# Attention beside a Fourier mix in one kernel: bursts of 6, 5 and 5 key chunks, half sums kept in DRAM, query tiles that stay in place

## The chip, the cores and the metric

The kernel runs on one core of a Trainium2 chip. The time is device microseconds (us) of one execution; the number compared is the median of several executions. Lower is better. The engines are named as in the profile: PE (TensorE matmuls; PEld its weight loads), DVE (VectorE), ACT (ScalarE), POOL (GpSimd) and SP (SyncE, which here only issues DMAs; its queue is written SPq).

## The reference

Two parts that share nothing; the output sets them side by side.

```python
# A: 2048 rows, D = 1024, 32 query heads of 32, one key head and one value head
q = (x @ wq) as 32 heads;  k = x @ wk;  v = x @ wv
p = softmax(q @ k.T * 32 ** -0.5)
a = concat_heads(p @ v) @ wo
# B: real part of a 2-D Fourier transform by matrices
re = xb @ dft_hid_re.T;  im = xb @ dft_hid_im.T
b = dft_seq_re @ re - dft_seq_im @ im
out = concatenate([a, b], axis=-1)          # 2048 x 2048
```

## The kernel before

**Attention.** A unit `u` is 512 queries times 4 heads; there are 32 units. A unit takes 32 steps in each of two passes. The score pass (`score_step`) computes a 128 x 1024 block of scores a step into `pss` (two buffers of the PSUM memory that PE writes), DVE takes its row maxima (`nm<-pss`) and ACT its exponentials and row sums. The second pass (`expo`), 44 steps behind, computes the scores again with keys on the partitions into `pst` (one buffer), and ACT writes their exponentials to a `p` tile: two `p` tiles for each chunk of 128 keys. A **burst** (`pv`) then multiplies several chunks' `p` tiles by the values: per chunk four matmuls with 32 columns of `v`, side by side in the PE array, into a `psb` bank. DVE adds the bank to the unit's sum `ov`. Before, every fourth chunk starts a burst: four of them a unit, at steps 8, 16, 24 and 32 (which is step 0 of the next unit).

**Products.** Everything else that PE multiplies (the query projections, the Fourier part in two stages, the output projection) is a list of `Group`s of float32 products, each split in three matmuls of reduced-precision halves: `rh,mh`, `rl,mh`, `rh,ml`. `take(n)` issues the next n of these matmuls; between the score and exp matmuls of each step `level` takes as many as bring the fill position `pos["fill"]` to its goal at the next burst. So a step is two `pss`, two `pst` and some product matmuls (five or six as a rule); a step with a burst takes none, except the few that `aside` needs to leave an opened or nearly closed group.

**Operands.** Left operands (`m`) and right operands (`r`) run through a `Line` of four steps: load from DRAM (on SP), sum of up to three sources (`comb`: POOL, `m<-m,m` and `r<-r,r`), high half (`mh`, `rh`: POOL cast), low half (`ml`, `rl`: POOL subtraction). `lead` says how many fill positions before its due time each step is issued; right operands had (40, 40, 14, 8). Right operands of a set are due one by one over the set before.

**The Fourier part's second stage** (`stage2`) works through `PRODUCTS`: seven products of summed blocks. Each is 16 groups of 24 product matmuls: eight row blocks `k` for the first half of the contraction, then eight for the second. A row of `PRODUCTS` holds the left operand's sources, the right operand's, and the outputs to which the product is added. The first half's result stayed in an SBUF tile `h` until the second half's group added to it (DVE, `h<-h,psb`); then POOL adds it to each output that exists already (`y<-y,h`, the earlier value having been loaded from DRAM) and SP stores it; an output's first value is stored as it is.

**Order.** `Ordered` records each engine's instructions in the order of the program, so an engine that waits holds up all that is behind it; SP is such a queue too. `open_unit` opens the next unit's query tile `qst` six steps ahead: a POOL memset of its last 32 partitions and three loads.

## Time and profile before

| | |
|---|---|
| three runs | 2765.34 us median, 2764.76 to 2766.59 |
| the profiled execution | 2764.96 us, of which the span from first to last instruction is 2762.9 us |
| granted TensorE clock | 1.000 |
| busy: PE / PEld / DVE / ACT / POOL | 2750.9 / 1927.0 / 1599.3 / 2173.0 / 1650.2 us |
| DMA | 458 MB, 166 GB/s in the mean |

Everything runs through one helper line (L66), so groups are told apart by their tiles: `out<-in`. Matmuls overlap in the pipeline: a row's duration is longer than the distance to the next start, and this distance is what a matmul costs PE. A float32 matmul of a burst is two instructions in the trace; a burst of four chunks is 4 x 4 x 2 = 32.

### The profile page before, as it was taken

Reading aid. Unit: us, or ns where it says so; the run is one execution under the profiler, and the core shown is the slowest. Engines: PE = TensorE matmul, PEld = TensorE weight load, DVE = VectorE, ACT = ScalarE, POOL = GpSimd, SP = SyncE. Lnnn points to the kernel's source line nnn. Section 1 sums busy time; section 2 is a strip of 40 time slices with the busy share of each in tenths; the row PEclk is TensorE's granted clock in tenths of the full one; section 3 lists DMA queues with packets and bytes.
Section 4 is the critical chain, followed back from the end, with each engine's and each line's share of the span. In section 5 each row is a group of like instructions: output and inputs, shape, how many; then the busy total and the mean of one; then the engine's idle time right before and its main releaser. Section 6 shows DMA issues by size and latency. Waiting matters only on the chain.

```text
span 2762.9 us, 39957 instructions
## 1 busy us (share of the span) xinstructions
PE 2750.9 (100%) x13868; PEld 1927.0 (70%) x13868; DVE 1599.3 (58%) x1830; ACT 2173.0 (79%) x3131; POOL 1650.2 (60%) x1620
## 2 busy tenths in 40 slices
PE   9999999999999999999999999999999999999999
PEld 6767676766767676676767677666676767677667
DVE  5766666666666665555555565555565555556411
ACT  3588788888888888888888888878888888888741
POOL 4845525655536447767785576798887885640110
PEclk9999999999999999999999999999999999999999
DMA  7643336765675555554463454555555552554455
GB/s 270 196 130 121 123 99 196 235 221 186 208 246 196 168 164 164 154 164 139 148 189 111 127 165 126 182 191 162 170 182 150 173 166 79 162 159 140 123 168 179
DMA packets 302473, 458.01 MB, mean 166 GB/s; under 512 B 31040, under 2 KB 96320, under 8 KB 302272
## 3 DMA queue, kind: packets, MB, share of 16 engines
q1 hardware_dynamic: 301120, 453.50, 52.7%
q8 instruction: 109, 1.79, 0.3%
q10 hardware_dynamic: 1152, 1.97, 0.2%
q14 instruction: 92, 0.75, 0.1%
HBM read 349.44 MB, written 104.60 MB: 164 GB/s over the span
## 4 chain that ended last, share of the span: by engine, by line
PE 97%; POOL 1%; DMA 1%; DVE 1%; issue 0%; ACT 0%; SPq 0%; POOLq 0%; ACTq 0%; DVEq 0%
PE psb L66 60%; PE pss L66 19%; PE pst L66 17%; POOL y L66 0%; DVE nm L66 0%; SPq L66 0%; DMA u<-y 0%; DVE y L66 0%; ACT p L66 0%; DMA p<-in_xT_dram 0%; POOL ml L66 0%; DMA m<-in_cT_dram 0%; DMA r<-s 0%; ACT pss L66 0%; POOL rl L66 0%
## 5 line engine op out<-in xcount | busy, mean ns | idle before, releaser
L66 DVE TENSOR_REDUCE nm<-pss 128x1 f32<-128x1024 f32 x1024 | 1252.5, 1223 | 576.8 <-PE pss L66 576.3
L66 ACT ACTIVATE p<-pst 128x1024 f32<-128x1024 f32 x1026 | 1052.7, 1026 | 457.9 <-PE pst L66 453.9
L66 ACT ACTIVATE pss<-pss,nm 128x1024 f32<-128x1024 f32 x1024 | 1112.3, 1086 | 63.1 <-DVE nm L66 61.1
L66 PE MATMUL psb<-rh,ml 128*128 128x512 f32 x1806 | 711.2, 394 | 3.7 <-POOL ml L66 3.7
L66 PE MATMUL psb<-rh,mh 128*128 128x512 f32 x1806 | 710.9, 394 | 0.4 <-ACT rh L66 0.4
L66 PE MATMUL psb<-rl,mh 128*128 128x512 f32 x1806 | 709.9, 393 | 0.8 <-DVE rl L66 0.8
L66 PE MATMUL pss<-kst,qst 128*128 128x512 f32 x2048 | 657.4, 402 | 0.1
L66 PE MATMUL pst<-qst,kst 128*128 128x512 f32 x2048 | 648.3, 397 | 0.9 <-ACT p L66 0.7
L66 PEld LDWEIGHTS pss<-kst,qst 128*128 128x128 f32 x2048 | 372.5, 188 | 182.9 <-issue 99.7
L66 PE MATMUL psb<-p,v 128*32 128x512 f32 x4096 | 466.0, 596 | 0.8 <-DVE y L66 0.8
L66 POOL TENSOR_TENSOR ml<-m,mh 128x512 fp32r<-128x512 f32 x338 | 436.3, 1291 | 33.8 <-ACT mh L66 26.4
L66 PEld LDWEIGHTS pst<-qst,kst 128*128 128x128 f32 x2048 | 379.4, 188 | 104.4 <-ACT p L66 16.0
L66 PEld LDWEIGHTS psb<-rh,ml 128*128 128x128 f32 x1806 | 339.4, 188 | 83.9 <-POOL ml L66 5.6
L66 PEld LDWEIGHTS psb<-rh,mh 128*128 128x128 f32 x1806 | 339.4, 188 | 82.9 <-ACT rh L66 2.1
L66 PEld LDWEIGHTS psb<-rl,mh 128*128 128x128 f32 x1806 | 339.4, 188 | 80.8 <-DVE rl L66 1.7
L66 POOL TENSOR_TENSOR r<-r,r 128x512 f32<-128x512 f32 x112 | 144.4, 1289 | 302.2 <-DMA r<-s 158.7
L66 PEld LDWEIGHTS psb<-p,v 128*32 128x32 f32 x4096 | 120.4, 110 | 276.7 <-issue 262.1
L66 POOL CAST mh<-m 128x512 fp32r<-128x512 f32 x337 | 206.4, 612 | 158.8 <-PE psb L66 141.2
L66 POOL CAST rh<-r 128x512 fp32r<-128x512 f32 x208 | 127.7, 614 | 249.9 <-PE psb L66 159.7
L66 POOL TENSOR_TENSOR rl<-r,rh 128x512 fp32r<-128x512 f32 x208 | 268.6, 1292 | 3.9
L66 POOL TENSOR_TENSOR m<-m,m 128x512 f32<-128x512 f32 x192 | 247.9, 1291 | 29.9 <-DMA m<-in_xbT_dram 21.4
L66 DVE TENSOR_TENSOR ov<-ov,psb 128x512 f32<-128x512 f32 x96 | 66.1, 688 | 288.7 <-PE psb L66 288.7
(91 smaller groups left out, 961.9 us busy)
## 6 DMA issues: line engine op xcount, KB each, us to landing
m<-in_cT_dram SPq DMA_DIRECT2D x384, 256.0 KB, 3.7
r<-s SPq DMA_DIRECT2D x192, 256.0 KB, 4.3
y<-y SPq DMA_DIRECT2D x96, 256.0 KB, 4.6
r<-in_wT_dram SPq DMA_DIRECT2D x80, 256.0 KB, 3.8
m<-in_xbT_dram SPq DMA_DIRECT2D x80, 256.0 KB, 4.1
y<-u SPq DMA_DIRECT2D x80, 256.0 KB, 2.9
m<-in_wq_dram SPq DMA_DIRECT2D x64, 256.0 KB, 3.1
qst<-qh SPq DMA_DIRECT2D x64, 256.0 KB, 5.3
```

The costliest lines, as they stand in the source:

```text
L66: return lambda *a, **k: self.tc.keep_in_program_order(f(*a, **k))
```

## The change

- `CUT = (0, 6, 11, NC)`: a unit's 16 chunks go in three bursts of 6, 5 and 5 chunks, at steps 12, 22 and 32. There are 96 bursts where there were 128. The pool of `p` tiles has 13 buffers instead of 9, and `level` spreads the product matmuls over 12 or 10 steps.
- Room for the 4 `p` tiles comes from the eight `h` tiles. The first half's sum goes to DRAM (`hs`, 56 stores) and comes back with the other old values (`part`, 56 loads, first in the list `ys`) into a `y` tile, to which DVE adds the second half.
- Third sources of a sum, which lay in `h` tiles, use the second source's two buffers (`r1`, `m1`); `may` lets an operand with three sources, and the one behind it, be loaded only when all sums before it are issued.
- Query tiles are three fixed ones. POOL clears each once (3 memsets instead of 32); for the other 29 units a DMA copies two rows of zeros over the two rows that the unit before wrote.
- `PRODUCTS`: the second row becomes the fourth.
- Right operands' sums are issued 28 positions ahead, not 40; their loads stay at 40.

```diff
 PRODUCTS = [
     ([(0, 0, 1), (1, 1, 1)], ((0, 0), (1, 1)), [(0, 0, 1), (1, 1, 1)]),
-    ([(0, 1, 1), (1, 1, 1)], ((0, 0),), [(1, 0, 1), (1, 1, -1)]),
     ([(0, 0, 1)], ((0, 1), (1, 1)), [(0, 1, 1), (1, 1, 1)]),
     ([(0, 0, 1), (1, 0, 1)], ((1, 1),), [(0, 0, 1), (0, 1, -1)]),
+    ([(0, 1, 1), (1, 1, 1)], ((0, 0),), [(1, 0, 1), (1, 1, -1)]),
...
         def may(self, k):
             if k == 0:
+                if self.n[1] < i and any(len(it.srcs) > 2 for it in self.items[i - 1:i + 1] if it.srcs):
+                    return False
...
-    RL = Line(NR0, NR, (40, 40, 14, 8), load_r, comb, hi_r, lo)
+    RL = Line(NR0, NR, (40, 28, 14, 8), load_r, comb, hi_r, lo)
...
                     if half == 0:
-                        def post(ps, k=k):
-                            hs[k] = hp.tile([P, W], F32, name=f"h{k}")
-                            dve.tensor_copy(hs[k], ps)
+                        def post(ps, k=k, hs=hs, f=f):
+                            o = op.tile([P, W], F32, name="qh")
+                            dve.tensor_copy(o, ps)
+                            store(hs[k], o, ("h", f, k))
                         yield Group(left, R, post)
                         continue
-                    ys = []
+                    part = Item([(lambda k=k, hs=hs, f=f: have(("h", f, k), hs[k]), 1)])
+                    ys = [part]
...
-                    def post(ps, k=k, plan=plan):
-                        h = hs[k]
+                    def post(ps, part=part, plan=plan):
+                        h = part.y
                         dve.tensor_add(h, h, ps)
...
-    qsp = pool(ctx, "qsp", 3)
-    pp = pool(ctx, "pp", 9)
+    qsp = pool(ctx, "qsp", 1)
+    rows = []
+    NP = 13
+    pp = pool(ctx, "pp", NP)
...
-        q = qsp.tile([P, 4, W], F32R, name="qst")
-        gp.memset(q[96:P].bitcast(F32), 0.0)
+        if u < 3:
+            rows.append(qsp.tile([P, 4, W], F32R, name=f"qst{u}"))
+            gp.memset(rows[u][96:P].bitcast(F32), 0.0)
+        q = rows[u % 3]
+        if u >= 3:
+            move(sp, q[96:98].rearrange("p a b -> p (a b)"), kst[98:100])
...
+    CUT = (0, 6, 11, NC)
...
-        for c in range(4 * k, 4 * k + 4):
+        for c in range(CUT[k], CUT[k + 1]):
...
+    ENDS = [2 * c for c in CUT]
     def level(n):
-        k, r = divmod(n, 8)
-        if r == 0:
+        r = n % SU
+        if r in ENDS:
             return
-        left = goal((k + 1) * 8) - pos["fill"]
-        take(left - left * (7 - r) // (8 - r))
+        more = min(e for e in ENDS if e > r) - r
+        left = goal(n + more) - pos["fill"]
+        take(left - left * (more - 1) // more)
...
-        if r % 8 == 0 and n:
-            pv(*divmod(n // 8 - 1, 4))
+        if r in ENDS and n:
+            pv((n - 1) // SU, (ENDS.index(r) - 1) % (len(CUT) - 1))
```

How the order of instructions changes is shown at three places. On PE, a burst in the second stage, with the step around it, before:

```order
L66 MATMUL psb<-rh,ml 128x512
L66 MATMUL psb<-ident,nm 48x128
L66 MATMUL pss<-kst,qst 128x512 x2
L66 MATMUL pst<-qst,kst 128x512 x2
L66 MATMUL psb<-p,v 32x512 x16
L66 MATMUL pss<-kst,qst 128x512 x2
L66 MATMUL pst<-qst,kst 128x512 x2
L66 MATMUL psb<-rh,mh 128x512
```

and a first burst of a unit there now:

```order
L66 MATMUL psb<-rh,ml 128x512
L66 MATMUL pss<-kst,qst_688 128x512 x2
L66 MATMUL pst<-qst_1988,kst 128x512 x2
L66 MATMUL psb<-p,v 32x512 x24
L66 MATMUL pss<-kst,qst_688 128x512 x2
L66 MATMUL pst<-qst_1988,kst 128x512 x2
L66 MATMUL psb<-rh,mh 128x512
```

The burst has 24 matmuls (6 chunks) instead of 16, and what stands around it is the same; the transposition `psb<-ident,nm`, which stood right before a unit's third burst, now stands two steps behind one.

On POOL, one group of the second half of the fourth product, before:

```order
L66 TENSOR_TENSOR y_17136<-y_17136,h_16285 128x512
L66 TENSOR_TENSOR y_17138<-y_17138,h_16285 128x512
L66 TENSOR_TENSOR m_17181<-m_17181,m_17183 128x512
L66 TENSOR_TENSOR ml<-m_17111,mh 128x512
L66 TENSOR_TENSOR r_17310<-r_17310,r_17312 128x512
L66 CAST mh<-m_17181 128x512
L66 CAST rh<-r_17176 128x512
L66 TENSOR_TENSOR m_17261<-m_17261,m_17263 128x512
L66 TENSOR_TENSOR ml<-m_17181,mh 128x512
L66 TENSOR_TENSOR rl<-r_17176,rh 128x512
L66 CAST mh<-m_17261 128x512
```

and at that place now:

```order
L66 TENSOR_TENSOR y_17104<-y_17104,y_17102 128x512
L66 TENSOR_TENSOR m_17140<-m_17140,m_17142 128x512
L66 TENSOR_TENSOR ml<-m_17078,mh 128x512
L66 CAST mh<-m_17140 128x512
L66 CAST rh<-r_17136 128x512
L66 TENSOR_TENSOR m_17188<-m_17188,m_17190 128x512
L66 TENSOR_TENSOR ml<-m_17140,mh 128x512
L66 TENSOR_TENSOR rl<-r_17136,rh 128x512
L66 TENSOR_TENSOR r_17278<-r_17278,r_17280 128x512
L66 CAST mh<-m_17188 128x512
```

One `y` addition a group is gone (the product that now stands fourth has one output that exists already; the one with two now stands third, where the next product's right operands need no sums), and the right operand's sum stands later among the left operands' steps.

On SP, the same place, before (`s` is stage one's result, `cT` the Fourier matrix):

```order
L66 DMA y_17286<-y_0_4_245 128x512
L66 DMA y_17288<-y_1_4_253 128x512
L66 DMA r_17310<-s_5_324 128x512
L66 DMA r_17312<-s_5_340 128x512
L66 DMA m_17315<-in_cT_dram 128x512
L66 DMA m_17317<-in_cT_dram 128x512
L66 DMA y_0_3_244<-y_17136 128x512
L66 DMA out_dram<-y_17138 128x512
```

and now:

```order
L66 DMA y_17212<-hs_3_407 128x512
L66 DMA y_17214<-y_1_3_268 128x512
L66 DMA qst_1316<-kst 2x2048
L66 DMA qst_1316<-qh_6_79 32x4x512
L66 DMA qst_1316<-ql_6_111 32x4x512
L66 DMA qst_1316<-qh_6_79 32x4x512
L66 DMA r_17278<-s_4_320 128x512
L66 DMA r_17280<-s_4_336 128x512
L66 DMA m_17282<-in_cT_dram 128x512
L66 DMA m_17284<-in_cT_dram 128x512
```

The half sum `hs` is loaded at the head of the group's loads, and the zeros for a query tile are a DMA ahead of its three loads.

More of the change, by code (lines that the diff above doesn't have):

```diff
@@ L132, in tile_kernel @@
     op = pool(ctx, "op", 3, side="right")
-    hp = pool(ctx, "hp", 1, side="right")
     def move(q, to, of):
@@ L184, in load_r @@
         for n, (ap, _) in enumerate(it.srcs):
-            if n < 2:
-                it.t.append(r0p.tile([P, W], F32, name=f"r{n}", bufs=NR0 - n))
-            else:
-                it.t.append(spare(0, 5))
+            k = min(n, 1)
+            it.t.append(r0p.tile([P, W], F32, name=f"r{k}", bufs=NR0 - k))
             sp.dma_start(it.t[-1], ap())
@@ L196, in load_m @@
             a = ap()
-            if n < 2:
-                t = m0p.tile([P, 4, P], F32, name=f"m{n}", bufs=NM0 - n)
-            else:
-                t = spare(5, 3).rearrange("p (a b) -> p a b", a=4)
+            k = min(n, 1)
+            t = m0p.tile([P, 4, P], F32, name=f"m{k}", bufs=NM0 - k)
             it.t.append(t[:, :a.shape[1], :a.shape[2]])
             sp.dma_start(it.t[-1], a)
-    turn = {0: 0, 5: 0}
-    def spare(first, n):
-        turn[first] += 1
-        return hp.tile([P, W], F32, name=f"h{first + turn[first] % n}")
     def comb(it):
@@ L481, in stage1 @@
                     yield Group(left, R[n], post, ys=ys, part=(R, 4 * n))
-    hs = {}
     def have(key, ap):
@@ L493, in stage2 @@
                 total[t, e] = total.get((t, e), 0) + 1
-        for mt, nt, outs in PRODUCTS:
+        for f, (mt, nt, outs) in enumerate(PRODUCTS):
+            hs = [dram.tile([P, W], F32, name=f"hs_{f}_{k}") for k in range(8)]
             for half in range(2):
@@ L690, in pv @@
         ps = bank("psb")
-        for c in range(4 * k, 4 * k + 4):
+        for c in range(CUT[k], CUT[k + 1]):
             for h in range(4):
-                te.matmul(ps[h * DH:(h + 1) * DH], v[:, c], pt[u, c, h // 2][:, h % 2], start=c == 4 * k, stop=c == 4 * k + 3)
+                te.matmul(ps[h * DH:(h + 1) * DH], v[:, c], pt[u, c, h // 2][:, h % 2], start=c == CUT[k], stop=c == CUT[k + 1] - 1)
         if k == 0:
@@ L699, in pv @@
         cur["at"] += 1
-        if k == NC // 4 - 1:
+        if k == len(CUT) - 2:
             b, g = units[u]
@@ L740, in tile_kernel @@
         te.matmul(ps_t.tile([P, 2, W], F32, name="pst")[:, 0, :n], zeros[:, :P], zeros[:, :n], start=True, stop=True)
-    room = [t[:, k] for t in [pp.tile([P, 2, W], F32, name="p") for _ in range(9)] for k in range(2)]
-    room += [hp.tile([P, W], F32, name=f"h{k}") for k in range(8)]
-    room += [t[:, k].bitcast(F32) for t in [qsp.tile([P, 4, W], F32R, name="qst") for _ in range(2)] for k in range(4)]
+    room = [t[:, k] for t in [pp.tile([P, 2, W], F32, name="p") for _ in range(NP)] for k in range(2)]
+    room += [r0p.tile([P, W], F32, name="r1", bufs=NR0 - 1) for _ in range(2)] + [onp.tile([P, W], F32, name="rb")]
+    room += [m0p.tile([P, 4, P], F32, name="m1", bufs=NM0 - 1).rearrange("p a b -> p (a b)") for _ in range(2)]
+    room += [r0p.tile([P, W], F32, name="r0", bufs=NR0)]
     xs = [[room[b * ND + c] for c in range(ND)] for b in range(NQ)]
@@ L813, in tile_kernel @@
     take(last[0].at - pos["fill"] - 12)
-    pv(len(units) - 1, 3)
+    pv(len(units) - 1, len(CUT) - 2)
     while ends:
```

## The prediction

> **What bounds the kernel.** I read the page's busy table and its chain first.

> ```profile
> span 2762.9 us, 39957 instructions
> PE 2750.9 (100%) x13868; PEld 1927.0 (70%) x13868; DVE 1599.3 (58%) x1830; ACT 2173.0 (79%) x3131; POOL 1650.2 (60%) x1620
> PE 97%; POOL 1%; DMA 1%; DVE 1%; issue 0%; ACT 0%; SPq 0%; POOLq 0%; ACTq 0%; DVEq 0%
> ```

> PE is idle for 12.0 us of the span (2762.9 - 2750.9), and 97% of the chain that ended last is PE. So an edit pays only if PE gets less to do, or if it closes one of the few waits of PE. The change leaves the number of matmuls as it is; what it can touch on PE is the cost of starting and ending a burst, and the waits. I sum against the profiled execution, 2764.96 us (2.1 us of it outside the span); the median of the runs, 2765.34, is 0.4 us above it. Under 0.2% (5.5 us) I would not tell a change from none.

> **Fewer bursts.** The timeline of PE shows a burst, then steps of six and of five product matmuls without one (start, duration, instruction; only starts matter, since matmuls overlap).

> ```profile
> 1002.48 0.63 PE L66 MATMUL pst<-qst,kst 128*128 128x512 f32 x2
> 1003.03 3.64 PE L66 MATMUL psb<-p,v 128*32 128x512 f32 x32
> 1006.60 0.73 PE L66 MATMUL pss<-kst,qst 128*128 128x512 f32 x2
> 1007.17 0.62 PE L66 MATMUL pst<-qst,kst 128*128 128x512 f32 x2
> ...
> 1009.02 0.63 PE L66 MATMUL pss<-kst,qst 128*128 128x512 f32 x2
> 1009.48 0.63 PE L66 MATMUL pst<-qst,kst 128*128 128x512 f32 x2
> 1009.95 0.40 PE L66 MATMUL psb<-rh,mh 128*128 128x512 f32 x1
> ...
> 1011.33 0.63 PE L66 MATMUL pss<-kst,qst 128*128 128x512 f32 x2
> ...
> 1013.42 0.63 PE L66 MATMUL pss<-kst,qst 128*128 128x512 f32 x2
> ```

> Two windows inside the burst show where a wave of four neighbouring matmuls starts, five waves apart; the third row, of the chain, is a longer run of column tiles (64 wide, 16 waves of two) at the kernel's start.

> ```profile
> 1003.48 1.04 PE L66 MATMUL psb<-p,v 128*32 128x512 f32 x8
> 1005.63 1.04 PE L66 MATMUL psb<-p,v 128*32 128x512 f32 x8
> 13.23 7.02 PE pss L66 x32
> ```

> A wave is (1005.63 - 1003.48) / 5 = 0.43 us, a chunk two waves, 0.86. Four chunks are 3.44. The burst costs more than that at three places. It starts 0.55 after the `pst` pair (1002.48 to 1003.03), where a product starts 0.47 after one (1009.48 to 1009.95): 0.08. From its start to the next `pss` pair 3.57 pass, 0.13 more than the eight waves. And this pair takes 0.57 (1006.60 to 1007.17) instead of 0.46 (1009.02 to 1009.48): 0.11. Together 0.32 us a burst. That the 0.13 doesn't grow with the length is shown by the 16 waves at the start: 7.02 - 16 x 0.43 = 0.14. The chunks stay 512, the bursts become 96 from 128: 32 x 0.32 = **-10.2 us**. Bounds: only the 0.08 of the entry goes (-2.6), or the whole 0.32 and a bit of unseen waiting too (0.35, -11.2). I take 0.32, because all three parts sit at a burst's ends.

> [...]

> **Longer stretches between bursts.** Nine or eleven steps now run between bursts instead of seven. A step with five product matmuls is 2.09 us (1011.33 to 1013.42), one with six 2.31 (1009.02 to 1011.33). ACT goes through the steps with five without a gap (`pss` exponentials between):

> ```profile
> 1014.55 1.02 ACT L66 ACTIVATE p<-pst 128x1024 f32<-128x1024 f32 x1
> ...
> 1016.64 1.03 ACT L66 ACTIVATE p<-pst 128x1024 f32<-128x1024 f32 x1
> ```

> Its turn is 2.09 (1014.55 to 1016.64), as long as PE's. So a step with four products could be bound by ACT. Two such steps before a burst:

> ```profile
> 1138.99 0.63 PE L66 MATMUL pst<-qst,kst 128*128 128x512 f32 x2
> 1140.86 0.63 PE L66 MATMUL pst<-qst,kst 128*128 128x512 f32 x2
> 1142.75 0.73 PE L66 MATMUL pst<-qst,kst 128*128 128x512 f32 x2
> ```

> They take 1.87 and 1.89, and only behind the second does the `pst` pair take 0.10 longer: ACT lags by one of its turns at most, and catches up in the burst. The order of the changed kernel has 41 such steps instead of 28, four times three in a row, which before has nowhere. A third one in a row may cost up to the whole 0.22 (2.09 - 1.87). Four of those, and a few more pairs at 0.10: **+1 us**. Bounds: 0, and 41 x 0.22 = +9.

> **POOL: the waits of PE that there are.** Rows of the list of waits (us in total, times, longest), of the DMA table and of the groups, a window (its length, then PE's busy time), POOL's timeline about the first wait of PE for it, and DVE's additions of half sums, one a group, where nothing jams:

> ```profile
> PE psb L66 <- POOL ml L66: 3.7, 4, 1.2
> POOL r L66 <- DMA r<-s: 158.7, 62, 8.9
> PEld pst L66 <- ACT p L66: 16.0, 67, 0.7
> r<-s SPq DMA_DIRECT2D x192, 256.0 KB, 4.3
> L66 POOL MEMSET qst<- 32x2048 f32 x32 | 57.8, 1805 | 1.8
> 1800.00:1850.00 50.00, 47.17 (x233) 32.90 (x232) 27.94 (x32) 38.87 (x57) 45.70 (x45) 1.00 0.63 201
> 1794.54 1.30 POOL L66 TENSOR_TENSOR r<-r,r 128x512 f32<-128x512 f32 x1 [4.88 <-DMA r<-s]
> 1795.77 0.61 POOL L66 CAST mh<-m 128x512 fp32r<-128x512 f32 x1
> ...
> 1801.18 2.55 POOL L66 TENSOR_TENSOR y<-y,h 128x512 f32<-128x512 f32 x2
> ...
> 1814.15 2.54 POOL L66 TENSOR_TENSOR y<-y,h 128x512 f32<-128x512 f32 x2
> ...
> 2022.68 0.69 DVE L66 TENSOR_TENSOR h<-h,psb 128x512 f32<-128x512 f32 x1 [0.38 <-PE psb L66]
> 2032.88 0.69 DVE L66 TENSOR_TENSOR h<-h,psb 128x512 f32<-128x512 f32 x1
> 2046.85 0.69 DVE L66 TENSOR_TENSOR h<-h,psb 128x512 f32<-128x512 f32 x1 [0.16 <-PE psb L66]
> ```

> PE waits four times for `ml`, 3.7 us in all; 2.8 us of its idle time lie between 1800 and 1850 (50 - 47.17): the second half of the fourth product, one operand after POOL's wait of 4.88. There POOL does per group eight sums or subtractions at 1.29 and three casts at 0.61, 12.2 us, and waits for a right operand's load besides (4.88 in the row). Two `y` pairs stand 13.0 us apart; a group of 24 products takes PE 12.1 where nothing jams (half of 2022.68 to 2046.85). POOL falls behind. The change takes one 1.29 out of the group (10.9 left), the memset of 1.80 out of every unit, and issues the sum 12 positions after its load: half a group, 6 us, against the 4.3 us that `r<-s` takes to land. So POOL gets some 10 to 15% room where it had none: **-3.7 us**. Bounds: 0 and -4.7 (four restarts of 0.1 and waits hidden in modelled ends). The other places are no fuller: the third product takes over two `y` additions, but its group has a right operand without a sum, 10.9 again. The sum comes 6 us nearer to its use; the low half behind it stays 8 positions ahead, so a late one would wait there, and PE shows no wait for POOL's `rl` now. The 52 us of memsets (29 x 1.80) are otherwise off PE's path.

> **Half sums through DRAM.** 56 stores and 56 loads on SP; 29 small DMAs of zeros. DVE now waits for a load before it adds, and the row maxima queue behind it. Issues of the loads that stand at the same place now (one for the addition at 2032.88 above), and an addition at the jam:

> ```profile
> 2024.97 0.43 SPq L66 DMA_DIRECT2D y<-y  x1
> ...
> 1839.01 0.90 SPq L66 DMA_DIRECT2D y<-y  x2
> 1844.34 0.69 DVE L66 TENSOR_TENSOR h<-h,psb 128x512 f32<-128x512 f32 x1
> y<-y SPq DMA_DIRECT2D x96, 256.0 KB, 4.6
> ```

> Issue (2024.97) is 7.9 us ahead of the addition (2032.88); landing takes 4.6 in the median, which leaves 3.3. At POOL's jam (1839.01, 1844.34) it is 5.3: just landed. Stage one already has DVE add to reloaded values, and its waits (the view of tile `y`) are

> ```profile
> L66 DVE TENSOR_TENSOR y<-y,psb x112: 628/684/690, 435.7 to 1035.7; 128x512 f32<-128x512 f32 x112
>   DMA u<-y: 0.2, 1
> ```

> 0.2 us in 112 additions. I take **0**, covered by the 3.3 us; upper bound in the rivals. Sums of three sources with two buffers: one such operand falls due every 24 products, 12.1 us, and needs a landing and two sums, 4.3 + 2.6: **0**. The zeros for a query tile go out six steps ahead: **0**. 32 fewer DVE additions of 0.69: off the path.

> **Sum:** 2765.0 - 10.2 + 1.0 - 3.7 = 2752.1, and 2752.5 against the median; I say **2752**.

> **Rivals.**
> - *POOL stays late, or another load is late in its place.* For: SP's queue, through which all operands come, gets 141 more issues. Against: 10.9 us of work in 12.1. Only the bursts pay, 2765 - 10.2 + 1: 2756.
> - *Only a burst's entry is saved*, the other two parts being restarts that follow the amount of work: 2765 - 2.6 - 3.7 + 1 = 2759.7. [...] Against: 0.14 at 16 waves.
> - *ACT binds the longer stretches*: every step of four at 2.09, +9: 2765 - 10.2 - 3.7 + 9 = 2760. For: the gapless rows. Against: 1.87 in steps with four.
> - *More is gained*: the upper bounds of bursts and POOL hold (-11.2, -4.7), the longer stretches cost nothing, and the bursts no longer wait for the transposition's bank, which stood right in front of one in each of 32 units: 2765 - 15.9 - 1 = 2748, with 1 us for that.
> - *Slower: the reloaded half sums come late.* DVE then stands before the row maxima of `pss`, ACT and PE behind it. Its slack a step:

> ```profile
> 1016.17 1.23 DVE L66 TENSOR_REDUCE nm<-pss 128x1 f32<-128x1024 f32 x1 [0.86 <-PE pss L66]
> ```

> 0.86 us. The gain of 12.9 is eaten, and 5.5 more, when each of 56 additions is late by 0.86 + 18.4 / 56 = 1.2 us; at 1.5 us it is 2752 + 36 = 2788. The loads would have to land 3.3 + 1.2 us later than those of before. For: the 5.3 at the jam. Against: the jam goes, and stage one's 0.2. [...]

> **Chances.** The forecast (2749 to 2754) 0.60; POOL stays late 0.14; entry only 0.06; ACT binds 0.08; more is gained 0.07; late half sums 0.05. Against 2765.3, faster by over 0.2% ends at 2759.8: forecast, POOL, more, and half of entry only, 0.84. Same: the other half, and ACT, 0.11. Slower 0.05. The range 2745 to 2760 leaves out the late half sums, part of ACT and some of the edges, under 2 in 10; the burst bounds (-2.6 to -11.2) and POOL's lie in it.

> **What the profile would show.** Right: `psb<-p,v` still x4096, in rows of x48 and x40, 5.29 and 4.43 us from start to the next `pss`; no wait of PE for POOL `ml` about 1800; POOL's 158.7 on `r<-s` well down; DVE waiting for `hs` loads under 1 us; PE busy down by some 9 us. Wrong: a first `pss` pair behind a burst that takes over 0.7; weight loads of `pst` waiting for ACT well above their 16.0 us; a row of DVE waits on DMA `y<-hs`; PE idle over 12 us.

## The result, and the profile after

The changed kernel takes 2752.82 us (median of four runs, 2752.35 to 2752.88) against 2765.97 for the kernel before in the same job: a ratio of 0.9953, 95% interval 0.9941 to 0.9964. That is 13.2 us less, between 10.0 and 16.3 by the interval. The profiled execution has a span of 2750.8 us at full clock, 12.1 less than before.

The page of the changed kernel, its span, busy times, chain and DMA total:

```profile
span 2750.8 us, 40206 instructions
PE 2742.4 (100%) x13868; PEld 1928.3 (70%) x13868; DVE 1579.5 (57%) x1798; ACT 2165.2 (79%) x3131; POOL 1596.6 (58%) x1591
DMA packets 318720, 487.88 MB, mean 177 GB/s; under 512 B 32890, under 2 KB 98170, under 8 KB 318458
PE 98%; ACT 1%; DVE 0%; DMA 0%; issue 0%; SPq 0%; ACTq 0%
```

PE is busy 8.5 us less (2750.9 to 2742.4) for the same 13868 matmuls, and idle 8.4 us instead of 12.0. So about 8.5 us lie in how PE's work is laid out and 3.6 in waits. POOL and DMA have gone from the chain. DMA moves 30 MB more, at no cost that this page shows.

The timeline of PE in the changed kernel, a burst of five chunks in the middle of the kernel (start, duration, instruction):

```profile
1099.39 0.62 PE L66 MATMUL pst<-qst,kst 128*128 128x512 f32 x2
1099.94 4.50 PE L66 MATMUL psb<-p,v 128*32 128x512 f32 x40
1104.37 0.73 PE L66 MATMUL pss<-kst,qst 128*128 128x512 f32 x2
1104.94 0.63 PE L66 MATMUL pst<-qst,kst 128*128 128x512 f32 x2
```

From the burst's start to the next `pss` pair 4.43 us pass, the figure forecast. The entry is again 0.55 behind the `pst` pair, and the pair behind the burst again takes 0.57. All three fixed parts are as they were with four chunks.

The list of waits of the changed kernel (us in total, times, longest):

```profile
DVE nm L66 <- PE pss L66: 589.1, 786, 1.1
POOL r L66 <- DMA r<-s: 23.6, 7, 12.6
PEld pst L66 <- ACT p L66: 21.6, 84, 0.8
POOL y L66 <- DMA y<-hs: 3.4, 1, 3.4
```

POOL's waits for the right operands' loads fell from 158.7 us in 62 places to 23.6 in 7. No row of PE or its weight loads waiting for POOL's `ml` is left, and DVE has no row for the `hs` loads. POOL waits once for a half sum, 3.4 us. The weight loads of `pst` wait for ACT 5.6 us more than before (21.6 to 16.0): the mark of the longer stretches, since the run with bursts of four below has 15.7. Two windows of the changed kernel, about the old jam (length, then busy time of PE, PEld, DVE, ACT, POOL; granted clock, DMA share, GB/s):

```profile
1600.00:1800.00 200.00, 200.00 (x1033) 139.48 (x1035) 115.21 (x132) 166.60 (x243) 157.85 (x156) 1.00 0.65 196
1800.00:1850.00 50.00, 50.00 (x244) 37.03 (x236) 29.90 (x29) 43.41 (x62) 43.06 (x42) 1.00 0.62 200
```

PE is busy for all of the 50 us in which it had lost 2.8, and POOL has 7 us to spare there.

### The profile page after: what moved, and what is told of

Its sections match the earlier page's. It is cut to its first block, busy times and chain, and to the rows that moved or that the text cites. A ratio compares the mean times of both kernels' runs of the same rounds, so it can differ in the third digit from the quotient of the medians.

```text
span 2750.8 us, 40206 instructions
## 1 busy us (share of the span) xinstructions
PE 2742.4 (100%) x13868; PEld 1928.3 (70%) x13868; DVE 1579.5 (57%) x1798; ACT 2165.2 (79%) x3131; POOL 1596.6 (58%) x1591
## 4 chain that ended last, share of the span: by engine, by line
PE 98%; ACT 1%; DVE 0%; DMA 0%; issue 0%; SPq 0%; ACTq 0%
PE psb L66 62%; PE pss L66 19%; PE pst L66 18%; ACT p L66 0%; ACT pss L66 0%; DMA p<-in_xT_dram 0%; DVE nm L66 0%; DMA u<-y 0%; DVE y L66 0%; SPq L66 0%; DVE qh L66 0%; DVE rl L66 0%; ACT rh L66 0%; DVE p L66 0%; ACT nm L66 0%
## 5 line engine op out<-in xcount | busy, mean ns | idle before, releaser
L66 DVE TENSOR_REDUCE nm<-pss 128x1 f32<-128x1024 f32 x1024 | 1252.6, 1223 | 589.9 <-PE pss L66 589.1
L66 ACT ACTIVATE p<-pst 128x1024 f32<-128x1024 f32 x1026 | 1053.3, 1027 | 456.1 <-PE pst L66 453.5
L66 ACT ACTIVATE pss<-pss,nm 128x1024 f32<-128x1024 f32 x1024 | 1111.3, 1085 | 59.6 <-DVE nm L66 57.8
L66 PE MATMUL psb<-rh,mh 128*128 128x512 f32 x1806 | 710.9, 394 | 1.5 <-ACT rh L66 1.0
L66 PE MATMUL psb<-rl,mh 128*128 128x512 f32 x1806 | 709.4, 393 | 0.6 <-DVE rl L66 0.5
L66 PE MATMUL psb<-rh,ml 128*128 128x512 f32 x1806 | 710.0, 393 | 0.0
L66 PE MATMUL pss<-kst,qst 128*128 128x512 f32 x2048 | 653.7, 400 | 0.1
L66 PE MATMUL pst<-qst,kst 128*128 128x512 f32 x2048 | 649.5, 398 | 1.0 <-ACT p L66 0.7
L66 PEld LDWEIGHTS pss<-kst,qst 128*128 128x128 f32 x2048 | 374.6, 188 | 159.9 <-issue 76.3
L66 PE MATMUL psb<-p,v 128*32 128x512 f32 x4096 | 459.3, 594 | 0.0
L66 POOL TENSOR_TENSOR ml<-m,mh 128x512 fp32r<-128x512 f32 x338 | 437.0, 1293 | 38.0 <-ACT mh L66 26.5
L66 PEld LDWEIGHTS pst<-qst,kst 128*128 128x128 f32 x2048 | 377.4, 188 | 108.1 <-ACT p L66 21.6
L66 PEld LDWEIGHTS psb<-rh,mh 128*128 128x128 f32 x1806 | 338.9, 188 | 86.9 <-issue 2.6
L66 PEld LDWEIGHTS psb<-rl,mh 128*128 128x128 f32 x1806 | 338.9, 188 | 80.9 <-DVE rl L66 1.6
L66 PEld LDWEIGHTS psb<-rh,ml 128*128 128x128 f32 x1806 | 338.9, 188 | 79.5
L66 POOL CAST mh<-m 128x512 fp32r<-128x512 f32 x337 | 207.1, 614 | 212.5 <-PE psb L66 182.4
L66 PEld LDWEIGHTS psb<-p,v 128*32 128x32 f32 x4096 | 123.2, 110 | 283.6 <-issue 275.4
L66 POOL CAST rh<-r 128x512 fp32r<-128x512 f32 x208 | 128.1, 616 | 286.9 <-PE psb L66 202.6
L66 POOL TENSOR_TENSOR m<-m,m 128x512 f32<-128x512 f32 x200 | 258.8, 1294 | 51.7 <-DMA m<-in_xbT_dram 28.8
L66 POOL TENSOR_TENSOR rl<-r,rh 128x512 fp32r<-128x512 f32 x208 | 268.6, 1292 | 3.9
L66 POOL TENSOR_TENSOR ov<-ov,rb 128x512 f32<-128x512 f32 x31 | 40.1, 1294 | 317.3 <-DVE ov L66 313.7
L66 POOL TENSOR_TENSOR r<-r,r 128x512 f32<-128x512 f32 x120 | 155.2, 1293 | 114.0 <-DMA r<-in_wT_dram 88.3
## 6 DMA issues: line engine op xcount, KB each, us to landing
m<-in_cT_dram SPq DMA_DIRECT2D x384, 256.0 KB
r<-s SPq DMA_DIRECT2D x192, 256.0 KB
y<-y SPq DMA_DIRECT2D x128, 256.0 KB
r<-in_wT_dram SPq DMA_DIRECT2D x88, 256.0 KB
m<-in_xbT_dram SPq DMA_DIRECT2D x88, 256.0 KB
y<-u SPq DMA_DIRECT2D x80, 256.0 KB
m<-in_wq_dram SPq DMA_DIRECT2D x64, 256.0 KB
qst<-qh SPq DMA_DIRECT2D x64, 256.0 KB
```

Of the source, the lines that this page charges most:

```text
L66: return lambda *a, **k: self.tc.keep_in_program_order(f(*a, **k))
```

## The experiments

The ratios below are to the kernel before, timed on the same chip in the same job; its medians there were 2764.8 to 2765.2 us. Differences from the changed kernel's 2752.8 are taken across jobs: the kernel before was at 2766.0 in that one, so a us or so of each is uncertain.

### The length of a burst

The changed kernel with bursts of four chunks (`burst4`), and with six bursts a unit (`burst3`). Everything else of the change stays.

```diff
-    CUT = (0, 6, 11, NC)
+    CUT = (0, 4, 8, 12, NC)            # burst4
+    CUT = (0, 3, 6, 8, 11, 14, NC)     # burst3
```

> The changed kernel (2752.8 us) with one line put back: four bursts of 4 chunks a unit, 128 in all; half sums in DRAM, order of products, lead and query tiles stay as changed. Theory A (all of a burst's fixed cost, 0.32 us, goes with each burst that is saved): 32 x 0.32 = 10.2 comes back, the 1 us for longer stretches goes: 2762. Rival B (only the entry of 0.08 goes with a burst): 2752.8 + 2.6 - 1 = 2754.4. PE shows no wait for POOL's ml near 1800 in either.

> The changed kernel with six bursts of 3, 3, 2, 3, 3 and 2 chunks a unit, 192 in all, 96 more than it has. Theory A: 96 x 0.32 = 30.7 more, 1 us less for long stretches: 2782.5. Rival B (0.08 a burst): 2752.8 + 7.7 - 1 = 2759.5. If a burst's cost follows the number of chunks and not of bursts, no change: 2752.

Measured: `burst4` 2760.35 us, 0.9983 (0.9974 to 0.9992); `burst3` 2779.92 us, 1.0054 (1.0040 to 1.0068). The 64 bursts between them cost 19.6 us, 0.306 each; the forecast had 0.32. A burst of three chunks in the timeline of `burst3`:

```profile
1005.80 2.78 PE L66 MATMUL psb<-p,v 128*32 128x512 f32 x24
1008.51 0.73 PE L66 MATMUL pss<-kst,qst 128*128 128x512 f32 x2
```

Three chunks take 2.71 us to the next pair, four 3.57 and five 4.43: 0.86 a chunk and a constant 0.13. The 32 bursts between `burst4` and the changed kernel are worth 7.5 us, 0.235 each. At 0.306 they would be 9.8, so the longer stretches give back about 2.3 us, if a burst costs the same between five or six chunks and four as between four and three.

### The half sums' way through DRAM

`half_sbuf` is `burst4` with the half sums kept in SBUF tiles as before (the shorter bursts leave room for them); `late_y` is the changed kernel with all reloads of old values, the half sums' too, issued later.

```diff
-            hs = [dram.tile([P, W], F32, name=f"hs_{f}_{k}") for k in range(8)]
+            hs = {}
...
-                            o = op.tile([P, W], F32, name="qh")
-                            dve.tensor_copy(o, ps)
-                            store(hs[k], o, ("h", f, k))
+                            hs[k] = hp.tile([P, W], F32, name=f"h{k}")
+                            dve.tensor_copy(hs[k], ps)
```

```diff
-        while ydone[0] < min(len(ylist), yused[0] + NY) and ylist[ydone[0]].due - 24 <= pos["fill"]:
+        while ydone[0] < min(len(ylist), yused[0] + NY) and ylist[ydone[0]].due - 12 <= pos["fill"]:
```

> The kernel with 128 bursts of 4 chunks and 9 p tiles, and the first half's sums in eight SBUF tiles as before; order of products, lead, query tiles and three-source sums stay as changed. It differs from the run with four bursts a unit only in the trip of the half sums through DRAM. Theory A (the trip is hidden): the same as that run, 2762, within 1.5 us. Rival C (56 stores and loads cost something on the path, hidden so far in the gain): 3 us or more below that run.

> The changed kernel with all loads of values to be added (half sums, old outputs, first stage's sums) issued 12 positions ahead of their group's end instead of 24, some 6 us later. In the changed kernel the loads of half sums are issued 7.7 (least) to 15.5 us (median) ahead of DVE's addition, and such a load lands in 4.6. Theory A (the lead sets the issue, and DVE waits only for what is late): some 18 of 168 additions come 1 to 3 us late, of which 0.86 is free: about 10 us more, 2763, with a row of DVE waits on those loads. Rival D (SP's queue sets the issue and the lead has no effect): 2753. Had the margin been 3.3 us throughout, as the prediction took it: 2.7 us late, 1.8 beyond the free 0.86, 56 times: 2850.

Measured: `half_sbuf` 2760.07 us, 0.9983 (0.9974 to 0.9991), the same as `burst4`: where POOL isn't late, the trip through DRAM is free. `late_y` 2790.63 us, 1.0090 (1.0077 to 1.0104): with half the lead it costs 37.8 us. The sign was expected, the size was four times the expected one. DVE's waits for half sums in `late_y`, and four windows at the longest:

```profile
DVE y L66 <- DMA y<-hs: 49.8, 22, 5.7
```

```profile
2190.00:2194.50 4.50, 4.50 (x21) 3.65 (x20) 0.38 (x1) 2.74 (x4) 4.50 (x4) 1.00 0.98 313
2194.50:2199.00 4.50, 0.41 (x2) 0.00 (x0) 2.87 (x3) 0.95 (x1) 3.00 (x4) 0.89 0.88 305
2199.00:2205.00 6.00, 5.70 (x14) 4.32 (x15) 1.84 (x3) 4.38 (x8) 6.00 (x7) 0.51 0.52 155
2205.00:2215.00 10.00, 10.00 (x69) 5.05 (x68) 4.01 (x5) 4.60 (x7) 8.28 (x9) 1.00 1.00 259
```

In the windows before and in the wait, DMA is 98% and 88% busy. The half sum lands late, DVE stands before the row maxima, and PE does 0.41 us of work in 4.5. Then PE runs six us at a granted clock of 0.51. I had priced the lateness by the median landing; here the load is late where the queues are full. Four waits of PE in this trace, whose mean granted clock is 0.995, are paid a second time in clock: they are followed by 23.9 us at half clock in all, in which PE does 19.9 us of work. At full clock that would take about 10 us less (an estimate from these two numbers), so about a quarter of the 37.8 is clock.

### POOL's edits, put back

Three edits took POOL out of PE's way: the order of the products, the right operands' sums 12 positions later, and 29 memsets turned into DMAs. I put them back into the changed kernel in these combinations; the rest of the change (three bursts, half sums in DRAM, fixed query tiles) stays.

```diff
-    ([(0, 1, 1), (1, 1, 1)], ((0, 0),), [(1, 0, 1), (1, 1, -1)]),   # fourth row of PRODUCTS
+    ([(0, 1, 1), (1, 1, 1)], ((0, 0),), [(1, 0, 1), (1, 1, -1)]),   # second: "order"
-    RL = Line(NR0, NR, (40, 28, 14, 8), load_r, comb, hi_r, lo)
+    RL = Line(NR0, NR, (40, 40, 14, 8), load_r, comb, hi_r, lo)     # "lead"
-            move(sp, q[96:98].rearrange("p a b -> p (a b)"), kst[98:100])
+            gp.memset(q[96:P].bitcast(F32), 0.0)                    # "memsets"
```

The order alone (`order_back`), the lead alone (`lead40`), the memsets alone (`memset`), and all three (`pool_back`):

> The changed kernel with the rows of PRODUCTS in their old order; sums of right operands 28 ahead, no memsets, longer bursts and half sums in DRAM stay. Theory E (POOL's room comes from all three of order, lead and memsets, and two are enough): POOL's group in the fourth product is 12.2 + 0.5 again against 12.1 of PE, but without waiting for the right operand's load; it falls behind by some 4 us over eight groups, less than its margin: PE waits for ml under 1 us, 2753. Rival F (the order alone closed the jam): the four waits return, 2752.8 + 3.7 = 2756.5.

> The changed kernel with right operands' sums issued 40 positions ahead again. Theory E: POOL's waits on the loads r<-s go from 24 us back towards 150 us, since it meets the sum as soon as the load is issued, but PE doesn't wait for POOL: 2753. Rival H (the lead closed the jam): PE waits 3 to 4 us for ml, 2756.

> The changed kernel with the memset of 32 partitions by POOL in place of the DMA of zeros, in all 32 units. Theory E: 52 us more of POOL's time, no wait of PE on it: 2753. Rival I (the memsets were what POOL lacked): PE waits for ml again, 2755 or more.

> The changed kernel with order of products, lead of 40 and one memset a unit all put back; longer bursts and half sums in DRAM stay. Theories E and F: POOL's jam of before returns, PE waits about 3.7 us for ml between 1790 and 1850: 2756.5. Rival G (the jam went because fewer bursts or fewer DVE additions left more time): no wait, 2753.

| put back | us | ratio (95%) |
|---|---|---|
| nothing | 2752.8 | 0.9953 (0.9941 to 0.9964) |
| order | 2752.2 | 0.9955 (0.9942 to 0.9967) |
| lead | 2755.4 | one run |
| memsets | 2754.0 | one run |
| all three | 2766.6 | 1.0006 (0.9997 to 1.0015) |

One edit put back costs 0 to 3 us; all three cost 13.8, as much as the whole change had gained. No theory of mine had said more than 4. The two single runs are read from their traces, by when the same matmul of PE starts there and in the changed kernel. With the memsets PE's last matmul starts 0.7 us later, all of it from the first 18 us; with the lead 2.7 us later, 1.1 of them from about 1851 and 1.6 from about 2036. With the lead alone POOL stands as in the kernel before, and PE waits 0.9 us for `ml`:

```profile
POOL r L66 <- DMA r<-s: 179.6, 63, 14.3
```

So POOL's standing costs PE little where POOL has time to make it up. Waits of `pool_back`, and windows at its first jam:

```profile
POOL r L66 <- DMA r<-s: 162.4, 63, 13.7
PEld psb L66 <- POOL ml L66: 12.6, 11, 2.7
PE psb L66 <- POOL ml L66: 8.1, 8, 2.3
DVE y L66 <- DMA y<-hs: 5.3, 3, 2.6
```

```profile
1793.00:1796.00 3.00, 0.73 (x2) 0.30 (x2) 1.02 (x4) 2.12 (x4) 3.00 (x4) 1.00 0.22 81
1796.00:1800.50 4.50, 4.27 (x12) 3.41 (x13) 1.23 (x1) 1.72 (x2) 4.50 (x6) 0.64 0.54 146
1800.50:1805.00 4.50, 4.50 (x35) 1.96 (x38) 2.59 (x8) 2.52 (x5) 2.55 (x3) 0.98 0.92 314
```

The jam of before is back, twice as large (8.1 us of PE waiting for `ml` instead of 3.7), and its first wait is followed by 4.5 us at a clock of 0.64. Two questions were left: does the DRAM trip or the longer burst make it larger, and which two of the three edits make it?

`pool_back_b4` is `pool_back` with bursts of four chunks, so that beside before it has the DRAM trip, the fixed tiles and the sums of three sources, but memsets, lead, order and bursts of before. `order_lead` puts back order and lead, `lead_memset` lead and memsets. `before_lead28` is the kernel before with only the lead changed:

```diff
-    RL = Line(NR0, NR, (40, 40, 14, 8), load_r, comb, hi_r, lo)
+    RL = Line(NR0, NR, (40, 28, 14, 8), load_r, comb, hi_r, lo)
```

> The kernel with all three of POOL's edits put back (order of products, lead of 40, a memset a unit) and bursts of 4 chunks; half sums still go through DRAM. The run with longer bursts and these three put back took 2766.6, 13.8 above the changed kernel; the run with bursts of 4 and the three edits kept, 2760.4. Theory J (POOL's jam costs PE more because the bursts are longer): the jam costs here what it did before, some 4.6: 2765. Rival K (it costs more because loads of half sums stand in SP's queue behind operands that POOL frees late): 2760.4 + 13.8 = 2774, with DVE waiting for y<-hs as there.

> The changed kernel with the order of products and the lead of 40 put back, without the memsets. Alone the order cost nothing (2752.2) and the lead 2.6 (one execution). Theory E (any two edits are enough): 2755. Rival L (order and lead together make the jam, the memsets only add to it): 10 or more back, 2763, PE waiting over 10 us for ml.

> The changed kernel with the lead of 40 and one memset a unit put back, the new order of products kept. Alone 2.6 and 1.2 (one execution each). Theory E: 2755 to 2757, with waits of PE for ml under 4 us. Rival M (POOL has no room at all without the lead): 2763.

> The kernel before with one number changed: right operands' sums 28 positions ahead instead of 40; old order of products, memsets, bursts of 4 and half sums in SBUF stay. Theory N (the lead is the edit that gives POOL its room): POOL's waits on r<-s fall from 159 to some 30 us, PE's waits for ml about 1800 go, 2765 - 4.6 = 2760.4, as with all three edits. Rival O (the lead works only together with the new order or without the memsets): 2763 to 2765, waits for ml still there.

| kernel | us | ratio (95%) |
|---|---|---|
| `pool_back_b4` | 2773.1 | 1.0028 (1.0017 to 1.0039) |
| `order_lead` | 2767.8 | 1.0006 (0.9997 to 1.0015) |
| `lead_memset` | 2758.3 | 0.9977 (0.9967 to 0.9986) |
| `before_lead28` | 2760.6 | 0.9984 (0.9975 to 0.9993) |

`order_lead` costs as much as all three, so the old order with the old lead makes the large jam; the memsets add nothing to it. With the new order they add some 3 us to the old lead (against its one run). `before_lead28` shows what the lead does alone. Its waits of POOL for right operands, and the 80 us that hold the jam of before, in the kernel before and in this one:

```profile
POOL r L66 <- DMA r<-s: 27.6, 8, 8.0
```

```profile
1780.00:1860.00 80.00, 76.31 (x390) 51.87 (x389) 43.48 (x50) 62.93 (x91) 70.76 (x66) 1.00 0.64 198
1780.00:1860.00 80.00, 80.00 (x411) 55.93 (x410) 46.81 (x53) 67.06 (x98) 79.80 (x76) 1.00 0.74 225
```

PE loses 3.7 us there in the kernel before and nothing now, though POOL is busy for 79.8 of 80 us: it had time enough, and lost it standing. One number in the kernel before gives 4.4 us. `half_sbuf`, which has all three edits and also the fixed query tiles and the sums of three sources, gives 4.9 (2760.1); so what the lead leaves to the others is within 0.5 us.

The same place in `order_lead` shows how the jam comes about. POOL's timeline, then that of SP's DMA issues, then SP's waits from 1785 to 1800:

```profile
1782.07 1.30 POOL L66 TENSOR_TENSOR m<-m,m 128x512 f32<-128x512 f32 x1
1783.32 1.31 POOL L66 TENSOR_TENSOR ml<-m,mh 128x512 fp32r<-128x512 f32 x1
1791.74 1.26 POOL L66 TENSOR_TENSOR r<-r,r 128x512 f32<-128x512 f32 x1 [7.11 <-DMA r<-s]
```

```profile
1782.62 1.36 SPq L66 DMA_DIRECT2D r<-s  x2
...
1789.47 2.45 SPq L66 DMA_DIRECT2D rb<-r  x4
1796.59 0.83 SPq L66 DMA_DIRECT2D m<-in_cT_dram  x2
1797.51 0.38 SPq L66 DMA_DIRECT2D y<-hs  x1
```

```profile
SPq L66 <- POOL ml L66: 4.3, 1, 4.3
```

The load goes out at 1782.62 and the sum starts at 1791.74, 9.1 us later; POOL comes to it at 1784.63 and stands 7.11 us. Behind it in POOL's order is the `ml` that PE needs, and that SP needs before it may load the next `m`. So SP issues nothing from 1791.92 to 1796.59, and the half sum's load waits behind it as well. The load is slow where the DMA engines are busy throughout: SP has just issued a query tile's loads, and from 1782 to 1792.5 the DMA engines are busy for 90% or more of every half us. In the changed kernel a load at this place is nearly as slow, with a DMA share of 1.04 from 1776 to 1785 (the same two views):

```profile
1776.31 1.81 SPq L66 DMA_DIRECT2D r<-s  x2
```

```profile
1779.61 1.34 POOL L66 TENSOR_TENSOR m<-m,m 128x512 f32<-128x512 f32 x1
1780.86 1.33 POOL L66 TENSOR_TENSOR ml<-m,mh 128x512 fp32r<-128x512 f32 x1
1782.11 1.34 POOL L66 TENSOR_TENSOR rl<-r,rh 128x512 fp32r<-128x512 f32 x1
1784.76 1.29 POOL L66 TENSOR_TENSOR r<-r,r 128x512 f32<-128x512 f32 x1 [1.31 <-DMA r<-s]
```

The sum starts 8.5 us after the issue of its sources, released by them, but POOL works ahead of it until 1783.45 and stands for 1.31 us only.

Why this jam costs more in the changed kernel than before is shown only in part. `pool_back_b4` is 8 us slower than before in the runs, 8.5 in its profile. Counted by when the same matmul starts in both traces, 2.5 of the 8.5 us are lost in the first 18 us, 3.3 from 1800 to 1870, 1.1 about 2040 and 1.6 from 2200 to 2231. The first 2.5 are no jam: PE's products still start 0.43 us apart at 11 us (11.40 and 11.83), where in the kernel before they are 0.23 apart at 7 us (7.00 and 7.23). These are about the paces that PE has in `late_y` at a granted clock of 0.51 (0.42) and of 1.00 (0.23); that the clock is the cause here as well is my inference, since the windows give 1.00 from 4 to 14 us in both traces. Waits of `pool_back_b4`:

```profile
POOL r L66 <- DMA r<-s: 146.0, 56, 8.8
PEld psb L66 <- POOL ml L66: 10.6, 8, 2.7
PE psb L66 <- POOL ml L66: 7.4, 7, 2.3
```

PE's wait for `ml` has doubled (3.7 to 7.4), while POOL waits for `r` no longer than before. The time of 2773.1 is the one forecast (2774) for loads of half sums that stand late in SP's queue. But DVE waits only 3.3 us for half sums here, and SP's wait for `ml` at the place above is 4.3 us in the kernel before too. The load there even takes longer before (issue 1784.25, sum 1794.54), yet PE's wait behind it is only 0.9 us, against 2.3 in `pool_back_b4`. The sums of three sources and the fixed tiles were not separated from the trip either: which of them makes the jam dearer stays open.

## Why the prediction was right, and where its terms were off

The forecast was 2752 in a range of 2745 to 2760; measured 2752.8.

- **Fewer bursts, -10.2.** Right in mechanism and size: 0.306 us a burst between `burst4` and `burst3` makes 9.8 for 32. The row of 16 waves at the kernel's start had shown rightly that the 0.13 doesn't grow with length. The rival "only the entry is saved" (2759.7) falls.
- **Longer stretches, +1.** Direction right, a little small: about 2.3, a difference of 9.8 and 7.5 that is good to a us or so. The place forecast shows it, the third step of four in a row. From the timeline of PE in the changed kernel:

```profile
883.30 0.63 PE L66 MATMUL pst<-qst,kst 128*128 128x512 f32 x2
885.20 0.73 PE L66 MATMUL pst<-qst,kst 128*128 128x512 f32 x2
887.21 0.73 PE L66 MATMUL pst<-qst,kst 128*128 128x512 f32 x2
```

  The steps take 1.90 and then 2.01 us: the third is 0.15 above an undisturbed 1.86, not the 0.22 at which I had bounded it, and so are all four of them (0.6 us). Over all 41 steps of four the mean is 1.91 against 1.86 undisturbed, 2.0 us in all; before it was 1.90 in 28, 1.0 in all. So 1 of the 2.3 us is seen there, and the other 1.3 was not located. "ACT binds" (+9) falls.
- **POOL, -3.7.** Right in size for the sum (-4.4 in `before_lead28`), wrong in whose it is. The step that failed is "POOL gets some 10 to 15% room where it had none", with the room counted from work taken away. The room was there, in POOL's waiting: in the kernel before, the later issue alone gives that much, without the 1.29 a group and without the memset.
- **The same term missed what the edits guard against.** Its lower bound, and the rival "POOL stays late" at 2756, said that the bursts' gain comes whatever POOL does. `pool_back` and `order_lead` are at 2766.6 and 2767.8. With POOL late, the rest of the change costs 8 us in the runs of `pool_back_b4` (6 in its profile without the first 18 us), and the bursts give back 6.5. The rival had its place right and its price 11 us too low.
- **Half sums through DRAM, 0.** Right (`half_sbuf` and `burst4`), as long as POOL isn't late. The margin of 3.3 us was that of one of the tighter additions: over all 56 in the changed kernel, the issue lies 15.5 us ahead in the median and 7.7 at least. The slower rival's mechanism is real, as `late_y` shows, and its condition (loads landing 4.5 us later) did not occur. Slow loads there were, but of right operands: at the jam one released its sum only 8.5 (changed kernel) and 9.1 us (`order_lead`) after its issue, against 4.3 in the median to landing, and in both the DMA engines are busy nearly throughout (a share of 1.04 in the changed kernel, 90% or more of every half us in `order_lead`).
- **The sum.** With the measured terms: 2765.0 - 4.4 (lead) + 0.3 (DRAM, `half_sbuf` to `burst4`) - 9.8 + 2.3 = 2753.4, against 2752.8. The terms -9.8 and 2.3 together are the measured step from `burst4` to the changed kernel, and 0.3 is that from `half_sbuf` to `burst4`; so what this sum tests is only whether the lead alone takes the kernel before as far as `half_sbuf`, and it leaves 0.5 us. The forecast's -12.9 had the bursts net of their stretches 1.7 us too high (9.2 for 7.5), POOL 0.7 too low and the trip 0.3 too cheap.

## What to carry to other kernels

In a queue that works in order, issue an operation later than its load by about the landing time (here 6 us, where landing takes 4.3 in the median and up to 9 at the jam). With equal leads the engine stands, which costs little where it has time to spare (lead alone put back, some 3 us) and much where it has none; through the buffers that it frees the DMA queue can stand as well. An edit that seems to bring nothing alone can be what lets another pay, so put the guards back together, not only one by one. A fixed cost per burst is best read at its ends and checked with a longer and a shorter burst.

## What the runs showed of the hardware that I had not expected

A wait of PE can be paid twice. Behind the wait of over 4 us in `late_y` the granted clock was 0.51 for six us, and product matmuls started 0.42 us apart instead of 0.23. In `pool_back` a wait of 2.3 us had the same effect (0.64 over 4.5 us), but in `pool_back_b4` a wait of the same length, from 1801.13 to 1803.40, cost no clock. Windows of 3.41 us show the difference, two of `pool_back` and then two of `pool_back_b4`:

```profile
1793.81:1797.22 3.41, 1.14 (x5) 0.86 (x5) 0.24 (x2) 1.30 (x4) 3.41 (x3) 1.00 0.02 5
1797.22:1800.63 3.41, 3.41 (x9) 2.63 (x8) 1.23 (x1) 1.85 (x2) 3.41 (x5) 0.50 0.75 201
```

```profile
1799.15:1802.57 3.42, 1.99 (x9) 1.15 (x7) 1.60 (x4) 3.23 (x6) 3.42 (x5) 1.00 0.47 173
1802.57:1805.98 3.41, 2.58 (x11) 2.13 (x12) 1.23 (x1) 0.98 (x2) 3.41 (x4) 1.00 0.41 113
```

```profile
2746.08:2749.49 3.41, 1.08 (x5) 0.55 (x3) 0.42 (x1) 0.38 (x1) 0.00 (x0) 1.00 0.23 77
2749.49:2750.80 1.31, 0.00 (x0) 0.00 (x0) 0.00 (x0) 0.00 (x0) 0.00 (x0) 0.50 0.00 0
```

So in these traces 2.27 us of idle time in a window of 3.41 were enough, and 1.43 were not.
